# An attention and MLP-mixer kernel on Trainium2: other places in the queues for the loads and the last matmuls of one weight

## The chip, the core and the metric

The kernel runs on one core of a Trainium2 chip. A core has five engines that run side by side, each with its own queue of instructions that it takes in order: TensorE (PE, matrix products; its weight loads are shown as PEld), VectorE (DVE), ScalarE (ACT), GpSimd (POOL) and SyncE (SP), which here only issues transfers. Engines wait for each other through semaphores. An instruction at the head of a queue that still has to wait holds everything behind it. The metric is the time of one execution in microseconds (us).

## The reference

Three stages in a row, all in fp32, on batches of 2 and a sequence of 448:

```python
# 1. causal attention, 12 heads of 64
scores = where(mask, -1e9, q @ k.T / sqrt(64))
attn   = exp(scores - max(scores));  attn /= sum(attn) + 1e-9
x      = (attn @ v) laid out as [batch, 448, 768]
# 2. token and channel mixer
h  = relu(x.T @ w_tok1) @ w_tok2           # 448x256, 256x448, over tokens
u  = x + h.T
x  = u + relu(u @ w_ch1) @ w_ch2           # 768x1536, 1536x768, over channels
# 3. gated MLP
h  = gelu_tanh(x @ w_in);  a, g = halves of h        # 768x1024
gated = a * (w_sg @ layernorm(g) * g_ln + b_sg)      # over tokens, 448x448
out = x + gated @ w_out
```

The weights of stage 2 arrive as 64-bit floats.

## The kernel before

Precision is kept by splitting each fp32 operand into a high and a low part and taking three products, high x high, high x low and low x high (`mm3`, L184 to L188). A 64-bit weight slice is loaded as raw words by SP (`wraw`, L113) and decoded on the chip: ScalarE converts the upper words (L127), VectorE shifts and joins the lower ones (L130, L131), ScalarE makes the high part `whi` (L140) and GpSimd the low part `wlo` (L101). There are two buffers for raw slices, three for the joined `wm`, three for `whi` and `wlo`.

Attention goes over 24 heads, 12 of batch 0 and then 12 of batch 1, in pairs. A head is worked off in two halves. For a half, PE makes a tile of scores S (`s_ps`, L345), VectorE adds the mask and takes the maxima (L350), ScalarE makes the bias from the maxima (L357) and the exponentials (L359) and casts them to 16 bits (L371), GpSimd makes the low part (L372), and SP transposes both by a DMA (L373, `pT<-hl`). PE then multiplies the transposed tile `pT` with V (L396 to L398; `x_ps`, 15 matmuls for a half). The scores of the next halves are made ahead of these products, so that the chain from maximum to transpose has time. After the products of two heads VectorE divides by the sums (`rd`, `xf`, L424 to L426), and ScalarE and GpSimd split the result into `xh` and `xl` (L429, L101, L435).

After every fourth head `token_mix` runs the token mixer for those 256 channels: 22 matmuls with w_tok1 (`a_ps`, L443, L444 and mm3), a relu and split (`ah`, `al`, L448), 20 matmuls with w_tok2 and transposes of x (`u_ps`, L459), and a split of the sum into `u_hi`, `u_lo` (L470).

When batch 0 is through attention, its u is complete, and the first product of the channel mixer can start for batch 0 while batch 1 is still in attention. Its result has 12 tiles; the first eight of batch 0, m = 0 to 7, are made beside the heads of batch 1. One is called an R tile here: 18 matmuls on one decoded slice `w_ch1[m]` (`r_ps`). `up_third` (L493) makes tiles 0 to 3 in thirds of six matmuls between heads, `up` (L512) makes tiles 4 to 7 whole after the loop over heads. All of this is written in program order; a list scheduler that models time then places instructions on the queues, and three things steer it: `tc.high_priority` shifts an instruction's rank, the number of buffers sets the earliest place, and `tc.issue_after(x)` puts the instructions in its block behind x in the order of issue. The last is an order only, and acts on the queues of the engines that the block uses.

The loads of the eight slices are steered by such a block. `marks[n]` is the transpose (on SP) of head n's last half; the load of slice m stands behind `marks[H - 2 + m]`, which is head 10 + m. Without this the scheduler would place loads as early as their buffers allow.

From the R tiles on, batch 0 and 1 run the rest of the channel mixer and the gated MLP, with PE as the engine that everything waits for.

Of the kernel before, what the change touches and what calls it, by code (L numbers as in the profile page):

```python
# [28 lines left out]
def mixer_kernel(  # L29
# [20 lines left out]
    H, D = 2 * H2, D2 // 2  # L50
# [4 lines left out]
    NQ = 4  # L55
# [6 lines left out]
    AHEAD = 4  # L62
    VAHEAD = 2
    LATER = 1500

    def f32(ap):
        return ap.bitcast(F32)
# [75 lines left out]
    def load_w(src, pool=wpool, bufs=3):  # L143

        k = src.shape[1]
        hi = pool.tile([P, WC // P, P], F32R, tag="whi", name="whi", bufs=bufs)[:, :k, :]
        lo = pool.tile([P, WC // P, P], F32R, tag="wlo", name="wlo", bufs=bufs)[:, :k, :]
        load64(hi.rearrange("p a f -> p (a f)"), lo.rearrange("p a f -> p (a f)"), src.rearrange("p a f -> p (a f)"))
        return hi, lo
# [31 lines left out]
    def mm3(ps, pairs, begun=False, ended=True):  # L181

        n, done = len(pairs), []
        for i, ((lh, ll), (rh, rl)) in enumerate(pairs):  # L184
            nc.tensor.matmul(ps, lh, rh, start=i == 0 and not begun, stop=False)  # L185
            nc.tensor.matmul(ps, lh, rl, start=False, stop=False)  # L186
            done.append(nc.tensor.matmul(ps, ll, rh, start=False, stop=ended and i == n - 1).ins)  # L187
        return done  # L188
# [26 lines left out]
    def tok(i):  # L215
        return slice(KW[i] - rows(i), KW[i])
# [3 lines left out]
    def channel_up(m, batches, pool, psum):  # L220

        wh, wl = load_w(w_ch1[m])
        for b in batches:
            us = slice(b * S, (b + 1) * S)
            pr = psum.tile([P, 512], F32, tag="d", name="r_ps")
            mm3(pr[:, :S], [((wh[:, c, :], wl[:, c, :]), (u_hi[c][b], u_lo[c][b])) for c in range(NCC)])
            r_done(m, b, pr, pool)

    def r_done(m, b, pr, pool):

        r = pool.tile([P, S], F32, tag=f"r{m}_{b}", name="r")
        nc.scalar.activation(r, pr[:, :S], AF.Relu, accum_out=rsum[:, b, m:m + 1])
        r_of[m, b] = r
# [17 lines left out]
    with ExitStack() as at:  # L251
# [12 lines left out]
        w1h = tokw.tile([P, NQ, T], F32R, name="w1h")  # L264
        w1l = tokw.tile([P, NQ, T], F32R, name="w1l")
# [172 lines left out]
        def token_mix(b, g, xf, xh, xl):  # L438
            N = GH * D
            pa = ps_a.tile([P, NT, N], F32, tag="a", name="a_ps")  # L440
            for t in range(NT):
                ts = slice(t * P, (t + 1) * P)
                nc.tensor.matmul(pa[:, t, :], w1h[:, 0, ts], xh[:, 0, :], start=True, stop=False)  # L443
                nc.tensor.matmul(pa[:, t, :], w1l[:, 0, ts], xh[:, 0, :], start=False, stop=False)  # L444
                mm3(pa[:, t, :], [((w1h[:, c, ts], w1l[:, c, ts]), (xh[:, c, :], xl[:, c - 1, :])) for c in range(1, NQ)], True)
            ah = xp.tile([P, NT, N], F32R, tag="ah", name="ah")
            al = xp.tile([P, NT, N], F32R, tag="al", name="al")
            nc.scalar.activation(ah, pa, AF.Relu)  # L448
            nc.vector.scalar_tensor_tensor(al, pa, 0.0, f32(ah), ALU.max, ALU.subtract)

            ws = slice(64, 64 + S) if b == 0 else slice(0, S)
            for e in range(N // P):
                cc = g * (N // P) + e
                cs = slice(e * P, (e + 1) * P)
                pu = ps_u.tile([P, 512], F32, tag="u", name="u_ps")
                first = True
                for t in range(NT):
                    for l, r in ((ah, w2h), (ah, w2l), (al, w2h)):
                        nc.tensor.matmul(pu[:, :S], l[:, t, cs], r[:, t, ws], start=first, stop=False, skip_group_check=True)  # L459
                        first = False  # L460
                nc.tensor.matmul(pu[:, b * 64:b * 64 + 64], xh[:, 0, cs], ident2, start=False, stop=False, skip_group_check=True)
                for c in range(1, NQ):
                    xc = xf[:, e, 2 * c - 1:2 * c + 1].rearrange("p h d -> p (h d)")
                    if b == 1 and c == NQ - 1:
                        o, idn = pu[:, :S].rearrange("p (a t) -> p a t", t=64)[:, ::6], ident_s
                    else:
                        o, idn = pu[:, b * 64 + tok(c).start:b * 64 + tok(c).stop], ident
                    nc.tensor.matmul(o, xc, idn, is_transpose=True, start=False, stop=c == NQ - 1, skip_group_check=True)
                us = slice(b * S, (b + 1) * S)
                nc.scalar.copy(u_hi[cc][b], pu[:, :S])  # L470
                nc.vector.tensor_sub(u_lo[cc][b], pu[:, :S], f32(u_hi[cc][b]))


        last, last_x, marks = [None], [None], []
        order = [(b, h) for b in range(B) for h in range(H)]
        qks, vss = {}, {}

# [14 lines left out]
        dense = list(range(NF0))  # L492
        thirds = []  # L493

        def up_third():

            if not thirds:
                m = dense.pop(0)
                with tc.issue_after(marks[H - 2 + m]), tc.high_priority(offset=-LATER):
                    wh, wl = load_w(w_ch1[m])  # L500
                pr = ps_e.tile([P, 512], F32, tag="d", name="r_ps")
                thirds.extend((m, pr, wh, wl, c) for c in range(0, NCC, 2))
            m, pr, wh, wl, c0 = thirds.pop(0)
            mm3(
                pr[:, :S],
                [((wh[:, c, :], wl[:, c, :]), (u_hi[c][0], u_lo[c][0])) for c in (c0, c0 + 1)],
                c0 > 0, not thirds,
            )
            if not thirds:
                r_done(m, 0, pr, rpool)  # L510

        def up():  # L512

            m = dense.pop(0)
            with tc.issue_after(marks[H - 2 + m]):
                channel_up(m, [0], rpool, ps_e)

        def decode_tok(c):
# [12 lines left out]
        for n, (b, h) in enumerate(order):  # L531
            if n > 0:
                prepare(n + AHEAD)
                prepare_v(n + VAHEAD)
            if n == GH - 1:
                for c in range(2, NQ):
                    load_tok(c)
                for c in range(NT):
                    load_tok2(c)
            if h % GH == 0:  # L540
                x = (
                    xp.tile([P, GH // 2, 7, D], F32, tag="xf", name="xf", bufs=2),
                    xp.tile([P, NQ, GH * D], F32R, tag="xh", name="xh"),
                    xp.tile([P, NQ - 1, GH * D], F32R, tag="xl", name="xl"),
                )
            if h % 2 == 0:
                it = pair(b, h // 2, h % GH // 2, qks[b, h // 2], x, b == 0 and h > 0)
            next(it, None)
            marks.append(last[0])
            if h % GH == GH - 1:  # L550
                token_mix(b, h // GH, *x)

            if b == 1 and h >= 3:
                for _ in range(1 if h < H - 3 else 2):
                    up_third()

        while dense:
            up()


    NDC = 4
# [348 lines left out]
```

## Time and profile before

| | |
|---|---|
| median of 3 timed runs | 416.0 us (414.38 to 416.13) |
| the profiled execution | 416.44 us, span 414.7 us |
| mean granted clock of TensorE | 0.988 |
| PE busy | 391.3 us, 94% of the span |
| DVE, ACT, POOL busy | 282.4, 250.4 and 202.5 us (68, 60 and 49%) |

The span runs from the first to the last instruction in the trace; 1.7 us of the profiled execution lie around it. Busy times of PE are those of overlapping matmuls counted once. A share of 94% is a mean over stages: where PE is full, no other engine's work costs anything; where it has gaps, the wait that ends last there counts. The granted clock is the share of full speed that TensorE was given; 1.00 is 2.4 GHz, and a value between 0.5 and 1.00 for a stretch is a mean over time at 2.4 and at 1.2 GHz.

### The profile page before, as it was taken

To read this page: it belongs to the slowest core of one execution; us is meant where nothing else is said; L and a number is where in the kernel's file an instruction comes from. 1 tells how busy PE (TensorE), PEld (TensorE's weight loads), DVE (VectorE), ACT (ScalarE), POOL (GpSimd) and SP (SyncE) were. 2 spreads that over 40 slices of the span, in tenths; PEclk is the share of its full clock that TensorE was granted. 3 is DMA by queue.
4 is the path that set the end of the run, shared out by engine and by line. 5 is a ranking of instruction groups with operands and counts; after the bars stand their busy time and mean duration, and the time that the engine had idled before them with its cause. 6 is when DMAs were issued, how large, how long until landed. Compare 5 with 4: busy or idle time off the path is not lost.

```text
span 414.7 us, 7332 instructions
## 1 busy us (share of the span) xinstructions
PE 391.3 (94%) x2622; PEld 267.9 (65%) x2622; DVE 282.4 (68%) x696; ACT 250.4 (60%) x483; POOL 202.5 (49%) x208
## 2 busy tenths in 40 slices
PE   5879899799898998999999999999999999999996
PEld 3447778588787887999889555555544445554554
DVE  6887866887785426444446787557898996469742
ACT  3988767787876555565679886344256556553210
POOL 3759864997686466062261447145121348315300
PEclk9999999799999999999999999999999999999999
DMA  7999899979997544466643313534623131100122
GB/s 220 246 238 232 161 206 271 246 186 236 265 247 140 137 112 144 163 217 229 207 149 102 90 65 114 186 107 134 222 73 90 51 103 51 52 2 0 68 92 107
DMA packets 61747, 61.77 MB, mean 149 GB/s; under 512 B 47888, under 2 KB 53264, under 8 KB 61712
## 3 DMA queue, kind: packets, MB, share of 16 engines
q1 hardware_dynamic: 61712, 61.32, 55.6%
q8 instruction: 20, 0.33, 0.3%
q14 instruction: 15, 0.12, 0.1%
HBM read 47.29 MB, written 2.75 MB: 121 GB/s over the span
## 4 chain that ended last, share of the span: by engine, by line
PE 25%; DVE 18%; ACT 12%; POOL 10%; DMA 9%; issue 8%; SPq 0%; POOLq 0%; ACTq 0%
DMA wraw<-in 7%; PE r_ps L186 5%; PE r_ps L185 5%; PE r_ps L187 5%; ACT r L172 3%; POOL hl L372 3%; PE o_ps L187 2%; PE o_ps L185 2%; PE o_ps L186 2%; DVE y L173 2%; DVE wm L131 2%; DVE w2m L131 1%; ACT wm L127 1%; PE u_ps L459 1%; POOL w L179 1%
## 5 line engine op out<-in xcount | busy, mean ns | idle before, releaser
L345 PE MATMUL s_ps<-k,q 128*128 128x64 f32 (+3 forms) x216 | 57.2, 405 | 11.5 <-DVE mx L350 4.8
L372 POOL TENSOR_TENSOR hl<-pe,hl 128x512 f16<-128x512 f32 x43 | 52.3, 1223 | 25.6 <-ACT hl L371 24.5
L101 POOL TENSOR_TENSOR wlo<-wm,whi 128x768 fp32r<-128x768 f32 x20 | 39.9, 1994 | 40.4 <-ACT whi L140 40.2
L185 PE MATMUL r_ps<-uh,whi 128*128 128x448 f32 x144 | 55.1, 383 | 0.0
L130 DVE TENSOR_SCALAR wm<-wm 128x768 int32<-128x768 int32 (+2 forms) x35 | 22.9, 655 | 46.9 <-ACT wm L127 46.9
L186 PE MATMUL r_ps<-ul,whi 128*128 128x448 f32 x144 | 53.9, 374 | 0.0
L187 PE MATMUL r_ps<-uh,wlo 128*128 128x448 f32 x144 | 53.0, 368 | 0.0
L185 PE MATMUL y_ps<-r,w 128*128 128x448 f16 x144 | 50.8, 353 | 0.0
L127 ACT ACTIVATE wm<-wraw 128x768 f32<-128x768 f32 (+2 forms) x35 | 27.8, 798 | 38.0 <-DMA wraw<-in 24.1
L186 PE MATMUL y_ps<-r,w 128*128 128x448 f16 x144 | 50.7, 352 | 0.0
L187 PE MATMUL y_ps<-r,w 128*128 128x448 f16 x144 | 50.6, 352 | 0.0
L345 PEld LDWEIGHTS s_ps<-k,q 128*128 128x128 f32 x216 | 32.2, 207 | 22.5 <-DVE mx L350 6.7
L350 DVE CUSTOM_DVE_ANT_0 pe<-s_ps,mask 128x192 f32<-128x192 f32 (+3 forms) x84 | 34.6, 441 | 7.2 <-PE s_ps L345 6.4
L246 POOL TENSOR_TENSOR y<-yt,ul 128x448 f32<-128x448 f32 x12 | 15.8, 1319 | 46.4 <-DVE yt L244 46.4
L359 ACT ACTIVATE pe<-pe,bias 128x448 f32<-128x448 f32 (+3 forms) x74 | 35.6, 525 | 0.4
L131 DVE SCALAR_TENSOR_TENSOR wm<-wraw,wm 128x768 int32<-128x768 int32 (+2 forms) x35 | 32.8, 938 | 0.7
L396 PE MATMUL x_ps<-vh,pT 128*128 128x65 f16 (+1 forms) x240 | 26.9, 201 | 3.1 <-DMA pT<-hl 3.0
L371 ACT CAST hl<-pe 128x512 f16<-128x512 f32 x43 | 26.3, 611 | 5.9 <-DMA pT<-hl 4.7
L185 PEld LDWEIGHTS r_ps<-uh,whi 128*128 128x128 f32 x144 | 27.3, 190 | 3.0 <-issue 0.4
L186 PEld LDWEIGHTS r_ps<-ul,whi 128*128 128x128 f32 x144 | 27.2, 189 | 3.1 <-issue 0.6
L187 PEld LDWEIGHTS r_ps<-uh,wlo 128*128 128x128 f32 x144 | 27.2, 189 | 2.7 <-issue 0.2
L179 POOL TENSOR_TENSOR w<-w2m,w 128x768 f16<-128x768 f32 x12 | 21.2, 1787 | 15.8 <-ACT w L178 11.2
(212 smaller groups left out, 1016.0 us busy)
## 6 DMA issues: line engine op xcount, KB each, us to landing
wraw<-in SPq DMA_DIRECT2D x36, 768.0 KB, 4.5
wraw<-in SPq DMA_DIRECT2D x14, 512.0 KB, 3.8
vr<-in SPq DMA_DIRECT2D x12, 320.0 KB, 4.0
k<-in SPq DMA_DIRECT2D x12, 224.0 KB, 3.7
q<-in SPq DMA_DIRECT2D x24, 112.0 KB, 4.0
out<-ob SPq DMA_DIRECT2D x11, 224.0 KB, 1.9
wraw<-in SPq DMA_DIRECT2D x3, 256.0 KB, 4.6
pT<-hl SPq DMA_TRANSPOSE x43, 4.0
```

Source lines behind the costliest of these rows:

```text
L101: nc.gpsimd.tensor_sub(lo, src, f32(hi))
L127: nc.scalar.activation(m, words.bitcast(F32)[:, :, 1], AF.Prelu, scale=2.0 ** -112, alpha=-(2.0 ** 32))
L131: nc.vector.scalar_tensor_tensor(mi, words[:, :, 0], 29, mi, ALU.logical_shift_right, ALU.bitwise_or)
L185: nc.tensor.matmul(ps, lh, rh, start=i == 0 and not begun, stop=False)
L186: nc.tensor.matmul(ps, lh, rl, start=False, stop=False)
L187: done.append(nc.tensor.matmul(ps, ll, rh, start=False, stop=ended and i == n - 1).ins)
L345: last_s[0] = nc.tensor.matmul(ps[:, o:o + m], qp[:, q0:q0 + P], k2[:, ks], start=True, stop=True).ins
L350: last_mx[0] = nc.vector.tensor_tensor_reduce(out=pe[:, cs], in0=ps[:, cs], in1=mask0 if i == 0 else mask[:, MASKS[i]], scale=-1.0 / math. ...
L359: nc.scalar.activation(pe[:, cs], pe[:, cs], AF.Exp, bias=bias[:, j:j + 1], scale=-1.0)
L371: nc.scalar.copy(hl[:, 0], pe)
L372: nc.gpsimd.tensor_sub(hl[:, 1], pe, hl[:, 0])
L396: nc.tensor.matmul(o, ph, vh[:, c, h, :D + 1], start=j == 0, stop=False)
```

## The change

A table `BEHIND` gives the head behind whose last transpose each of the eight loads of w_ch1 for batch 0 is queued: 12, 15, 17, 18, 19, 20, 21, 22 in place of 10, 11, ..., 17. And the last two whole R tiles (m = 6 and 7) get a place on PE: the matmuls of m = 6 stand behind the last product with V (`last_x[0]`), those of m = 7 behind the last product with w_tok1 (`last_a[0]`, which is newly recorded). The computation is the same.

```diff
--- before.py
+++ after.py
@@ -62,6 +62,7 @@
     AHEAD = 4
     VAHEAD = 2
     LATER = 1500
+    BEHIND = [12, 15, 17, 18, 19, 20, 21, 22]
 
     def f32(ap):
         return ap.bitcast(F32)
@@ -442,7 +443,8 @@
                 ts = slice(t * P, (t + 1) * P)
                 nc.tensor.matmul(pa[:, t, :], w1h[:, 0, ts], xh[:, 0, :], start=True, stop=False)
                 nc.tensor.matmul(pa[:, t, :], w1l[:, 0, ts], xh[:, 0, :], start=False, stop=False)
-                mm3(pa[:, t, :], [((w1h[:, c, ts], w1l[:, c, ts]), (xh[:, c, :], xl[:, c - 1, :])) for c in range(1, NQ)], True)
+                amm = mm3(pa[:, t, :], [((w1h[:, c, ts], w1l[:, c, ts]), (xh[:, c, :], xl[:, c - 1, :])) for c in range(1, NQ)], True)
+            last_a[0] = amm[-1]
             ah = xp.tile([P, NT, N], F32R, tag="ah", name="ah")
             al = xp.tile([P, NT, N], F32R, tag="al", name="al")
             nc.scalar.activation(ah, pa, AF.Relu)
@@ -471,7 +473,7 @@
                 nc.vector.tensor_sub(u_lo[cc][b], pu[:, :S], f32(u_hi[cc][b]))
 
 
-        last, last_x, marks = [None], [None], []
+        last, last_x, last_a, marks = [None], [None], [None], []
         order = [(b, h) for b in range(B) for h in range(H)]
         qks, vss = {}, {}
 
@@ -496,7 +498,7 @@
 
             if not thirds:
                 m = dense.pop(0)
-                with tc.issue_after(marks[H - 2 + m]), tc.high_priority(offset=-LATER):
+                with tc.issue_after(marks[BEHIND[m]]), tc.high_priority(offset=-LATER):
                     wh, wl = load_w(w_ch1[m])
                 pr = ps_e.tile([P, 512], F32, tag="d", name="r_ps")
                 thirds.extend((m, pr, wh, wl, c) for c in range(0, NCC, 2))
@@ -509,10 +511,10 @@
             if not thirds:
                 r_done(m, 0, pr, rpool)
 
-        def up():
+        def up(behind=None):
 
             m = dense.pop(0)
-            with tc.issue_after(marks[H - 2 + m]):
+            with tc.issue_after(marks[BEHIND[m]]), tc.issue_after(behind) if behind else nullcontext():
                 channel_up(m, [0], rpool, ps_e)
 
         def decode_tok(c):
@@ -555,7 +557,7 @@
                     up_third()
 
         while dense:
-            up()
+            up({2: last_x[0], 1: last_a[0]}.get(len(dense)))
 
 
     NDC = 4
```

The queue of SP in the middle of attention, from the transposes of the first halves of a pair of heads on. `k2` and `q0` are loads for a later pair, `wraw` raw slices of w_ch1, `pT` transposes. Before:

```order
L113 DMA wraw_1667<-in_5 128x768
L113 DMA wraw_1932<-in_5 128x768
...
L298 DMA k2_1463<-in_1 128x448
L373 DMA_TRANSPOSE pT_1343<-hl_1344 128x8x128
L373 DMA_TRANSPOSE pT_1378<-hl_1379 128x8x128
L300 DMA q0_163<-in_0 64x448
L113 DMA wraw_2228<-in_5 128x768
L373 DMA_TRANSPOSE pT_1404<-hl_1405 128x8x128
L373 DMA_TRANSPOSE pT_1433<-hl_1434 128x8x128
```

After (its lines are numbered one or two higher):

```order
L299 DMA k2_1463<-in_1 128x448
L374 DMA_TRANSPOSE pT_1343<-hl_1344 128x8x128
L374 DMA_TRANSPOSE pT_1378<-hl_1379 128x8x128
L301 DMA q0_163<-in_0 64x448
L114 DMA wraw_1667<-in_5 128x768
L374 DMA_TRANSPOSE pT_1404<-hl_1405 128x8x128
L374 DMA_TRANSPOSE pT_1433<-hl_1434 128x8x128
```

The slices m = 0 (`wraw_1667`) and m = 1 (`wraw_1932`) stood ahead of four transposes more than now; m = 0 has the place of m = 2 (`wraw_2228`), and m = 1 and m = 2 come further down.

The queue of ScalarE in the same place: `wm` is the conversion of a slice, `bias`, `pe` and `hl` the steps of a half head, `uh` and `xh` splits of the token mixer, `vh` of V. Before:

```order
L371 CAST hl_1405<-pe0_155 128x512
L127 ACTIVATE wm_1666<-wraw_1667 128x768
L357 ACTIVATE bias_1429<-mx_1423 128x2
L359 ACTIVATE pe_1422<-pe_1422,bias_1429 128x192
L359 ACTIVATE pe_1422<-pe_1422,bias_1429 128x320
L371 CAST hl_1434<-pe_1422 128x512
L470 CAST uh2_0_98<-u_ps_932 128x448
L127 ACTIVATE wm_1931<-wraw_1932 128x768
```

After:

```order
L372 CAST hl_1405<-pe0_155 128x512
L358 ACTIVATE bias_1429<-mx_1423 128x2
L360 ACTIVATE pe_1422<-pe_1422,bias_1429 128x192
L360 ACTIVATE pe_1422<-pe_1422,bias_1429 128x320
L372 CAST hl_1434<-pe_1422 128x512
...
L322 ACTIVATE vh1_177<-vr_1316,sv_1322 128x10x64
L128 ACTIVATE wm_1666<-wraw_1667 128x768
L358 ACTIVATE bias_1487<-mx_1482 128x2
```

The conversion of slice 0 has moved from ahead of one half head's bias to ahead of the next one's (`bias_1487`), and that of slice 1 has left this place.

The end of attention on PE: `x_ps` are the last products with V, `r_ps_2544` and `r_ps_2575` the R tiles m = 6 and 7, `a_ps` the products with w_tok1, `u_ps` those with w_tok2. Before:

```order
L398 MATMUL x_ps_2248<-vh1_177,pT_2375 128x65
L186 MATMUL r_ps_2544<-ul4_0_114,whi_2534 128x448
L187 MATMUL r_ps_2544<-uh4_0_102,wlo_2535 128x448
...
L185 MATMUL r_ps_2575<-uh0_0_94,whi_2565 128x448
...
L187 MATMUL r_ps_2575<-uh5_0_104,wlo_2566 128x448
L443 MATMUL a_ps_2405<-xh_2083,w1h_151 128x256
...
L187 MATMUL a_ps_2405<-xh_2083,w1l_152 128x256
L459 MATMUL u_ps_2432<-w2h_153,ah_2428 128x448
```

After:

```order
L399 MATMUL x_ps_2248<-vh1_177,pT_2375 128x65
L186 MATMUL r_ps_2544<-uh0_0_94,whi_2534 128x448
...
L188 MATMUL r_ps_2544<-uh5_0_104,wlo_2535 128x448
L444 MATMUL a_ps_2405<-xh_2083,w1h_151 128x256
...
L188 MATMUL a_ps_2405<-xh_2083,w1l_152 128x256
L186 MATMUL r_ps_2575<-uh0_0_94,whi_2565 128x448
...
L188 MATMUL r_ps_2575<-uh5_0_104,wlo_2566 128x448
L461 MATMUL u_ps_2432<-w2h_153,ah_2428 128x448
```

Before, 13 matmuls of m = 6 stood ahead of the last products with V and five of m = 6 and 18 of m = 7 behind them; now 18 of m = 6 stand behind them, and the 18 of m = 7 between the products with w_tok1 and those with w_tok2.

## Rows read from the trace of the kernel before

**Rows 1.** The page's busy tenths in 40 slices of the span, PE.

```profile
PE   5879899799898998999999999999999999999996
```

**Rows 2.** Windows: us, busy us (x count) of PE PEld DVE ACT POOL, PEclk, DMA share, GB/s.

```profile
70.00:84.50 14.50, 12.15 (x119) 9.46 (x118) 12.13 (x36) 11.79 (x25) 12.16 (x14) 0.76 1.10 261
84.50:104.70 20.20, 20.20 (x202) 16.74 (x200) 15.23 (x41) 15.26 (x34) 16.79 (x21) 1.00 0.89 207
...
155.00:169.00 14.00, 12.17 (x83) 10.70 (x82) 7.15 (x9) 5.89 (x11) 7.57 (x8) 1.00 0.56 170
169.00:240.00 71.00, 71.00 (x356) 59.80 (x355) 39.40 (x76) 51.84 (x98) 26.78 (x14) 1.00 0.51 163
```

**Rows 3.** Timeline of PE: start, us, engine, line, out<-in [idle before <-releaser].

```profile
75.75 1.02 PE L345 MATMUL s_ps<-k,q 128*128 128x448 f32 x2 [2.00 <-DVE mx L350]
```

**Rows 4.** Timeline of SP's queue, 63 to 101 us.

```profile
63.77 1.05 SPq L113 DMA_DIRECT2D wraw<-in  x2
...
67.08 5.50 SPq L373 DMA_TRANSPOSE pT<-hl  x2
...
73.38 0.47 SPq L113 DMA_DIRECT2D wraw<-in  x1
73.94 4.76 SPq L373 DMA_TRANSPOSE pT<-hl  x2
...
87.63 4.97 SPq L373 DMA_TRANSPOSE pT<-hl  x3
...
99.22 1.06 SPq L113 DMA_DIRECT2D wraw<-in  x2
100.40 6.57 SPq L373 DMA_TRANSPOSE pT<-hl  x2
```

**Rows 5.** Timeline of ScalarE, 68 to 79 us.

```profile
68.93 0.91 ACT L127 ACTIVATE wm<-wraw 128x768 f32<-128x768 f32 x1 [1.69 <-DMA wraw<-in]
...
75.73 0.20 ACT L357 ACTIVATE bias<-mx 128x2 f32<-128x2 f32 x1
...
78.89 0.90 ACT L127 ACTIVATE wm<-wraw 128x768 f32<-128x768 f32 x1 [2.02 <-DMA wraw<-in]
```

**Rows 6.** Timeline of VectorE, near 70 us.

```profile
69.87 0.56 DVE L130 TENSOR_SCALAR wm<-wm 128x768 int32<-128x768 int32 x1 [2.48 <-ACT wm L127]
```

**Rows 7.** Tiles: pT whole, pT from 99 to 108 us, wraw whole.

```profile
L373 SPq DMA_TRANSPOSE pT<-hl x43: 1231/1247/4565, 11.2 to 148.5; - x43
...
DMA to landing us min/median/max: 3.0/4.0/9.1
...
DMA to landing us min/median/max: 8.1/8.6/9.1
...
DMA to landing us min/median/max: 3.1/4.3/7.1
```

**Rows 8.** Timeline of PE: four waits.

```profile
109.51 0.20 PE L396 MATMUL x_ps<-vh,pT 128*128 128x65 f16 x1 [1.69 <-DMA pT<-hl]
...
133.39 0.20 PE L396 MATMUL x_ps<-vh,pT 128*128 128x65 f16 x1 [1.31 <-DMA pT<-hl]
...
161.22 0.39 PE L443 MATMUL a_ps<-xh,w1h 128*128 128x256 f32 x1 [0.68 <-POOL xh L101]
...
165.54 0.48 PE L459 MATMUL u_ps<-w2h,ah 128*128 128x448 f32 x1 [0.69 <-ACT ah L448]
```

**Rows 9.** Lines, 60 to 170 us: xcount | busy, mean ns | idle before, releasers.

```profile
L101 POOL TENSOR_TENSOR wlo<-wm,whi 128x768 fp32r<-128x768 f32 x11 | 20.9, 1903 | 6.8 <-ACT whi L140 6.5
...
L131 DVE SCALAR_TENSOR_TENSOR wm<-wraw,wm 128x768 int32<-128x768 int32 x13 | 15.8, 1213 | 0.2
...
L127 ACT ACTIVATE wm<-wraw 128x768 f32<-128x768 f32 x13 | 11.8, 908 | 13.2 <-POOL wlo L101 6.8 <-DMA wraw<-in 6.2
...
L140 ACT CAST whi<-wm 128x768 fp32r<-128x768 f32 x11 | 9.1, 825 | 1.1 <-DVE wm L131 0.6 <-PE r_ps L186 0.5
```

**Rows 10.** Timeline of GpSimd, near 159 us.

```profile
158.93 1.84 POOL L101 TENSOR_TENSOR wlo<-wm,whi 128x768 fp32r<-128x768 f32 x1
```

## The prediction

> **What bounds the kernel now.** I read the page's slices first [rows 1]. TensorE (PE) is full in most; where it isn't is at the start, which this change doesn't touch, and in single slices between about 70 and 170 us. Next I read the busy times by stage [rows 2]. From 169 us on PE has no idle microsecond for 71 us at a clock of 1.00; 356 matmuls in 71.00 us are 0.20 us each. From there on the order of the program is the same in both kernels, so time can only be won or lost ahead of that point, in the second half of attention: 70 to 169 us. There PE loses time in four places, and the reader is to see a different cause in each.
>
> First, 70.0 to 84.5 us: 12.15 us busy of 14.50, so 2.35 idle, at a granted clock of 0.76 of the full one [rows 2]. That is a mixture of its two levels, 2.4 and 1.2 GHz; PE had waited 2.00 us for the maxima of score tiles (L350 on VectorE) [rows 3] before the slow time. 0.24 of 14.50 us are 3.5 us of full-speed work that wasn't done. The place costs 2.35 + 3.5 = 5.8 us. The reason stands on the other queues. SP issued two slices of w_ch1 at 63.77 [rows 4]; ScalarE's queue then stood 1.69 us at its conversion of the first one (L127) until that load landed, with a bias and exponentials of a running head queued behind it, and VectorE 2.48 us at the next step of the same slice (L130) [rows 5, 6]. A third slice, issued at 73.38, held ScalarE another 2.02 us at 78.89, in front of a head's cast (L371) [rows 4, 5]. The two transposes begun at 67.08 took SP 5.50 us, where the median transpose takes 1.25 [rows 4, 7].
>
> Second, near 107 us PE waited 1.69 us for a transposed tile pT [rows 8]. Two slices had gone out at 99.22, directly ahead of two transposes at 100.40 [rows 4]; those landed 8.1 and 9.1 us after their issue, the median being 4.0 [rows 7]. Third, near 133: 1.31 us, again for a pT [rows 8]. Fourth, 155 to 169: 14.00 - 12.17 = 1.83 us [rows 2], in waits after the last products with V: 0.68 for xh, 0.69 for ah [rows 8], and the rest, 0.46, for xl between them.
>
> **The change part by part.** No instruction is added or removed; eight loads, what decodes them, and two R tiles (18 matmuls each) move.
>
> *Loads behind later heads.* In the first place the two loads at 63.77 go, and the first slice is issued at the place of the third, between two pairs of transposes. What leaves this stretch is, twice over, one slice's decode: 0.91 (L127) and 0.83 (L140) on ScalarE, 0.56 (L130) and 1.21 (L131) on VectorE, 1.90 (L101) on GpSimd [rows 6, 9]; and the two waits of 1.69 and 2.48 us. But one wait stays, and I work it out. SP's transposes start at 67.08 as before; unheld they take 2 x 1.25, and the q load behind them 0.8 (67.08 + 5.50 to 73.38), so the first slice is issued at about 70.4 and lands, at the median of 4.3 [rows 7], near 74.7. L127 stands in ScalarE's queue ahead of the bias of the next head and ends near 75.6; that bias ran at 75.73 before [rows 5]. So the first half of this head gains nothing there. What gains is everything behind: the third slice's wait of 2.02 us in front of its cast goes, so the casts come 1.5 us sooner for the first half, and more for the second, whose cast stood behind a further L140. PE meanwhile has 60 matmuls with V and 22 with w_tok1 to do, for which it needn't wait for the new head. I take 3.5 of the 5.8 us. Its ends: 5.8, if the clock doesn't fall at all; and -2.0, if the slice lands later and ScalarE stands as long as at 78.89 while nothing covers it.
>
> In the second place the pair at 99.22 is gone: one transpose now stands ahead of the third slice, the next one behind a single slice. I take 1.2 of the 1.69 us; ends 0 (the transposes stay as late as now; with fewer loads in front they have no reason to be later) and 1.69.
>
> In the third place and up to 155 us the loads become denser, since the last five slices stand behind heads 18 to 22. Every load still has a transpose queued behind it on SP, and the last head's transpose now has two in front. I leave the wait of 1.31 us where it is.
>
> *The last two R tiles.* The seventh tile had 13 of its 18 matmuls ahead of the last products with V; now all 18 stand behind them. That takes 13 x 0.20 = 2.6 us of cover from the last transpose. In the kernel before nothing waited there. The last cast now has the eighth slice's L127 and the seventh's L140 just ahead of it, so the transpose will be later; I charge 1.0 us, with 0 and 2.6 as ends (the nearest row is the 1.31 us of the third place).
>
> The tail: before, 23 R matmuls (4.6 us) stood between the last V product and the products with w_tok1 (call them A); they covered all but 0.68 us of the chain rd, xf, xh, which so took 5.3. Now 18 stand there (3.6 us). The chain itself changes: a wlo of 1.84 us stood between the two halves of xh on GpSimd [rows 10]; now it stands ahead of all of them and can run while VectorE still makes xf. VectorE has one more L131 (1.21) in its way. So xh should be ready 5.3 - 1.84 = 3.5 to 4.7 us after the last V product, a wait of 0 to 1.1; with what is left of the 0.46 for xl I take 0.6 us in place of 1.15. The eighth tile now stands between A and the products with w_tok2 (U), 3.6 us over a wait of 0.69: that wait goes. 1.83 - 0.6 = 1.2 us gained; ends 0 and 1.8.
>
> **The sum.** -3.5 - 1.2 + 1.0 - 1.2 = -4.9 us. The profiled execution took 416.44 us (span 414.7), so 411.5 by that; from the median of the three timed runs, 416.0, it is 411.1. I take 411.3.
>
> By the Trainium skill (DMA: Bandwidth & Descriptors, section Queues, rings and completion order) each DMA engine takes the descriptors of a ring in the order in which they were put there. The 8.1 and 9.1 us of the second place agree with it. By that rule a transpose behind a slice pays for that slice wherever the slice stands, and since all eight still stand in front of transposes it speaks against this change; what it would give here is the second rival.
>
> **The rivals.** *All of it goes* (chance 0.15). If the clock stays at 1.00 through 70 to 85 us and the later loads collide with nothing, the four places give 5.8 + 1.69 + 1.31 + 1.83 = 10.6 us: 405.8. For it speaks that the other engines have slack: VectorE, ScalarE and GpSimd are busy 15 to 17 of 20.2 us in a stretch where PE is full [rows 2]. Against it: one slice still lands in the first stretch in front of a head.
>
> *Spread, not removed* (0.20). The heads of batch 1 stand behind the same eight decodes, in the same in-order queues, and each slice delays the next transposes. The first place then gives back later what it gains, since PE, once ahead, runs into pT tiles that come no sooner: three transposes in a row took SP 4.97 us at 87.63 with no slice near [rows 4], so attention's own pace is not far from PE's. Only the tail's 1.2 us stays, less the 1.0: 416 us. For it also: the single slice at 73.38 ahead of a pair of transposes went with 4.76 us on SP for the two [rows 4].
>
> *Late weights* (0.10), the case on the other side. From issue to wlo a slice needs 4.3 + 0.91 + 0.56 + 1.21 + 0.83 + 1.90 = 9.7 us [rows 6, 7, 9], and PE eats one R tile in 3.6. A tile whose slice is issued only two tiles' time ahead (7.2 us) waits 2.5 us. The last five loads stand behind five heads in a row, so the tiles of slices five to eight could each wait about 1.7: 6.8 us lost and 1.0 at the last transpose, against 3.5 + 1.2 won earlier and nothing left of the tail's gain: 3 us slower, 419. It decides if PE waits over 6 us in sum between the fourth tile and the first whole tile of batch 1. Against it: before, with loads far ahead, ScalarE waited 6.8 us in this stretch for GpSimd to free buffers [rows 9], so some of the lead was not used.
>
> **How the numbers follow.** Forecast 0.50, its own range 408.5 to 414; the three rivals 0.15, 0.20, 0.10; 0.05 lies between the first rival and the forecast. Half a per cent, about what a measurement of this kernel can tell from no change, is 2.1 us: faster is below 413.9, slower above 418.1. Faster: nearly all of the forecast, the first rival and the rest, 0.67. Same: the second rival and the forecast's upper end, 0.23. Slower: 0.10. The range for 8 in 10 reaches to the first two rivals: 406 to 416.3.
>
> **What would show it.** Right: no wait of ScalarE at L127 near 69 us; PE idle plus slow clock at 70 to 85 under 3 us; the wait for pT near 107 us shorter than 0.5; no wait for ah before the last U; PE full from about 164 us on, 5 us sooner than 169. Wrong: ScalarE standing at L127 for more than 3 us near 73 to 76 us, a second half-clock stretch between 75 and 100 us, or PE waiting for a wlo or for the last pT longer than 2.6 us. The forecast falls as a whole if the last U ends within 1 us of 169 us, or later.

## The result: slower, and the profile after

The changed kernel takes 419.6 us (median of 5 runs, 417.87 to 420.44) against 415.6 for the kernel before in the same comparison: ratio 1.0104, 95% interval 1.0082 to 1.0126. On another chip, in e9 below, it is 1.0118 (1.0063 to 1.0172). It is 1% slower where 1.1% faster was forecast. The profiled execution has a span of 417.6 us, 2.9 more than before. Medians and ratios here and below leave out the few executions that ran in a slower state (one each of e1, e6, e9 and e12, two of e8).

The page's slices of the kernel after, busy tenths of PE and the granted clock, to be read beside [rows 1]:

```profile
PE   5879889998988977999999999999999999999996
PEclk9989999999998996999999999999999999999999
```

The dip that stood in slice 8 has gone; a deeper one has come in slices 15 and 16. Busy times by stage of the kernel after (us, then busy us and count of PE, PEld, DVE, ACT, POOL, then PEclk, DMA share, GB/s):

```profile
70.00:84.50 14.50, 13.78 (x152) 11.47 (x151) 11.52 (x42) 11.02 (x26) 10.77 (x16) 1.00 0.97 200
84.50:104.70 20.20, 18.84 (x192) 15.33 (x191) 13.18 (x42) 15.12 (x38) 14.36 (x19) 1.00 0.90 181
104.70:130.00 25.30, 22.15 (x210) 19.04 (x210) 17.36 (x39) 19.64 (x41) 18.29 (x20) 0.96 0.87 196
130.00:150.50 20.50, 20.50 (x170) 17.85 (x169) 11.72 (x21) 11.73 (x22) 13.37 (x12) 0.97 0.91 237
150.50:171.50 21.00, 16.38 (x87) 14.84 (x82) 6.29 (x11) 8.24 (x15) 10.80 (x9) 0.84 0.50 168
171.50:242.50 71.00, 71.00 (x357) 59.90 (x356) 41.53 (x76) 51.53 (x98) 26.47 (x14) 1.00 0.49 162
```

and the stages of the kernel before that [rows 2] doesn't have:

```profile
104.70:130.00 25.30, 23.49 (x199) 20.09 (x198) 19.77 (x48) 19.59 (x45) 18.55 (x20) 1.00 1.05 235
130.00:155.50 25.50, 24.19 (x219) 21.42 (x218) 9.44 (x22) 14.81 (x31) 14.17 (x13) 1.00 0.58 119
155.50:168.80 13.30, 11.47 (x74) 10.11 (x70) 6.95 (x9) 5.89 (x11) 7.07 (x8) 1.00 0.51 169
```

The last products with V end at 150.5 us after and 155.5 before: 5.0 us sooner. 2.6 of these are the 13 R matmuls that now stand behind them (13 x 0.20), so by these two profiles attention itself won 2.4. From there to the first R tile of batch 1 it takes 21.0 us against 13.3. With 0.20 us for each of the 36 R matmuls in it (23 before), what isn't R takes 13.8 against 8.7: 5.1 lost. -2.4 + 5.1 = +2.7 of the 2.9 us. The 5.1 us repeat: e9, the same kernel in another execution, takes 21.1 us for that stretch. The 2.4 don't: seven kernels whose queues have the same order up to that point (the kernel after, e9, e1, e2, e3, e13 and e14 below) reached the last product with V between 148.8 and 154.5 us, so a gain of 2.4 from one profile isn't shown. What is clear of that spread is the loss at the end of attention.

PE's waits from 148 to 172 us in the kernel after (engine, line, waited for: us in total, times, longest), where the kernel before waited 0.68 for xh and 0.69 for ah [rows 8] and, as the last line here shows, 0.47 for xl:

```profile
PE a_ps L444 <- POOL xh L102: 3.7, 1, 3.7
PE a_ps L187 <- POOL xl L102: 0.9, 1, 0.9
```

```profile
162.31 0.39 PE L186 MATMUL a_ps<-xl,w1h 128*128 128x256 f32 x1 [0.47 <-POOL xl L101]
```

The chain behind the longer one stands on three queues. Timelines of the kernel after (start, us, engine, line, out<-in [idle before <-releaser]); VectorE:

```profile
153.23 0.56 DVE L131 TENSOR_SCALAR wm<-wm 128x768 int32<-128x768 int32 x1 [3.15 <-ACT wm L128]
153.71 0.22 DVE L425 TENSOR_SCALAR rd<-x_ps,sv 128x7 f32<-128x7 f32 x1
153.84 0.95 DVE L132 SCALAR_TENSOR_TENSOR wm<-wraw,wm 128x768 int32<-128x768 int32 x1
154.71 0.19 DVE L426 RECIPROCAL rd<-rd 128x7 f32<-128x7 f32 x1
154.94 0.62 DVE L427 TENSOR_TENSOR xf<-x_ps,rd 128x448 f32<-128x448 f32 x1
```

ScalarE:

```profile
152.29 0.91 ACT L128 ACTIVATE wm<-wraw 128x768 f32<-128x768 f32 x1 [2.71 <-DMA wraw<-in]
153.10 0.82 ACT L141 CAST whi<-wm 128x768 fp32r<-128x768 f32 x1
```

GpSimd:

```profile
154.00 2.45 POOL L102 TENSOR_TENSOR wlo<-wm,whi 128x768 fp32r<-128x768 f32 x1 [1.81 <-ACT whi L141]
156.42 0.56 POOL L436 TENSOR_SCALAR xh<-xf 64x64 fp32r<-64x64 f32 x2
157.06 1.08 POOL L102 TENSOR_TENSOR xh<-xf,xh 64x64 fp32r<-64x64 f32 x2
```

The conversion at 152.29 is that of the third slice loaded for batch 1; its R tile comes only at about 178.7 us (171.5 and two tiles of 3.6). Its raw words landed 2.71 us after ScalarE was ready for it. VectorE's next step of the same slice stands ahead of rd, so rd starts 3.2 us after the last product with V. Behind the conversion on ScalarE stands the whi of the first such slice, and GpSimd's wlo waits for that whi, ahead of xh's rows. In the kernel before rd started within 0.3 us of that product (155.55):

```profile
155.78 0.22 DVE L424 TENSOR_SCALAR rd<-x_ps,sv 128x7 f32<-128x7 f32 x1 [1.68 <-PE x_ps L398]
```

PE did R tile m = 6 in the meantime, then stood. Two stretches of the kernel after, and the first matmul of A and the first behind A, show the rest of the loss:

```profile
150.50:158.20 7.70, 3.99 (x27) 3.33 (x22) 3.06 (x7) 4.39 (x8) 5.59 (x6) 1.00 0.72 246
158.20:165.40 7.20, 6.28 (x26) 5.85 (x27) 1.77 (x3) 1.96 (x4) 3.36 (x2) 0.53 0.35 118
```

```profile
158.19 0.39 PE L444 MATMUL a_ps<-xh,w1h 128*128 128x256 f32 x1 [3.71 <-POOL xh L102]
164.09 0.57 PE L186 MATMUL r_ps<-uh,whi 128*128 128x448 f32 x1
```

After a stretch in which it was busy 3.99 of 7.70 us, TensorE ran at 0.53 of its full clock for 7.2 us. The waits are 4.63 us in place of 1.84, which is 2.8 more. The 22 matmuls of A took 5.0 us without their wait for xl (158.19 to 164.09, less 0.92); in the kernel before they took 3.2 at a clock of 1.00 (161.22 to 164.85, less 0.47). The first three R matmuls behind A took 0.37 us each in place of 0.20. That is 1.8 + 0.5 = 2.3 us for the slow clock, and 2.8 + 2.3 = 5.1, what was lost.

What ScalarE's conversions waited for tells why the slices are late. Its group in the kernel after, 60 to 172 us (count | busy, mean ns | idle before and releasers):

```profile
L128 ACT ACTIVATE wm<-wraw 128x768 f32<-128x768 f32 x13 | 11.7, 902 | 17.8 <-DMA wraw<-in 14.4 <-POOL wlo L102 3.4
```

In [rows 9] the same group waited 6.8 us for GpSimd (a buffer) and 6.2 for loads. Now it waits 14.4 for loads: the lead of the loads was used up.

### The profile page after: what moved, and what is told of

Read it like the earlier page. It is cut to its first block, busy times and chain, and to the rows that moved or that the text cites. A ratio compares the mean times of both kernels' runs of the same rounds, so it can differ in the third digit from the quotient of the medians.

```text
span 417.6 us, 7332 instructions
## 1 busy us (share of the span) xinstructions
PE 391.7 (94%) x2622; PEld 268.9 (64%) x2622; DVE 281.8 (67%) x696; ACT 250.3 (60%) x483; POOL 202.3 (48%) x208
## 4 chain that ended last, share of the span: by engine, by line
PE 29%; DVE 19%; DMA 16%; POOL 13%; ACT 12%; issue 10%; SPq 0%; POOLq 0%; ACTq 0%; DVEq 0%
DMA wraw<-in 10%; DMA pT<-hl 4%; PE r_ps L188 4%; PE r_ps L186 4%; PE r_ps L187 4%; ACT r L173 3%; PE s_ps L346 3%; POOL hl L373 3%; PE o_ps L188 2%; PE o_ps L187 2%; PE o_ps L186 2%; DVE pe L351 2%; DVE y L174 2%; DVE wm L132 2%; DVE w2m L132 1%
## 5 line engine op out<-in xcount | busy, mean ns | idle before, releaser
L131 DVE TENSOR_SCALAR wm<-wm 128x768 int32<-128x768 int32 (+2 forms) x35 | 23.2, 664 | 41.8 <-ACT wm L128 41.8
```

## The experiments

Three theories: A, the loss is made at the end of attention, where decodes of slices that land late stand ahead of rd and xh; B, it is the cover that the two R tiles took away; C, it is made earlier, by the first loads, in new waits between 75 and 130 us. Each ratio is to the kernel before on the same chip, with its 95% interval.

| run | loads behind heads | tiles placed | time, us | ratio |
|---|---|---|---|---|
| e9, the kernel after | 12, 15, 17, 18, 19 to 22 | yes | 420.0 | 1.0118 (1.0063 to 1.0172) |
| e3 | the same | no | 419.3 | 1.0097 (1.0062 to 1.0133) |
| e10 | the same, the eighth behind 21 | yes | 419.9 | 1.0108 (1.0055 to 1.0161) |
| e4 | 10 to 17, as before | yes | 416.0 | 1.0005 (0.9974 to 1.0037) |
| e5 | 10 to 13, 19 to 22 | yes | 416.1 | 1.0009 (0.9988 to 1.0031) |
| e6 | 12, 15, 17, five times 18 | yes | 414.4 | 0.9959 (0.9929 to 0.9988) |
| e11 | as e6 | no | 415.5 | 0.9995 (0.9962 to 1.0028) |
| e2 | as after, rd ahead on VectorE | yes | 422.3 | 1.0148 (1.0107 to 1.0189) |
| e13 | as after, xh ahead on GpSimd | yes | 420.4 | 1.0083 (1.0050 to 1.0116) |
| e14 | as after, both | yes | 417.6 | 1.0040 (1.0006 to 1.0074) |
| e1 | as after, both and ScalarE | yes | 416.8 | 1.0022 (0.9990 to 1.0053) |
| e7 | as before, all three | yes | 415.5 | 0.9993 (0.9964 to 1.0021) |
| e8 | as e6, all three | yes | 415.3 | 0.9990 (0.9956 to 1.0023) |
| e12 | as e6, the fifth slice's decode later | yes | 420.1 | 1.0105 (1.0050 to 1.0161) |

**The two halves of the change.** e3 leaves out the places of the tiles, e4 leaves out the later loads:

```diff
# e3, from the kernel after
-            up({2: last_x[0], 1: last_a[0]}.get(len(dense)))
+            up()
# e4, from the kernel after
-    BEHIND = [12, 15, 17, 18, 19, 20, 21, 22]
+    BEHIND = [10, 11, 12, 13, 14, 15, 16, 17]
```

> The kernel after with the loads behind later heads, and no place given to the last two R tiles: on PE the 18 matmuls of m = 7 stand between the last products with V and A, m = 6 stays where it is. Theory A: the late chain is the same (xh ready 7.6 us after the last product with V), but 3.6 us more of R cover it; PE waits under 1 us for xh, about 1 us for xl and 0.7 for ah, and TensorE isn't slowed: 413 to 415. Theory B: the loads by themselves gain what was forecast for them, 411 to 412.

> The kernel before with the places of the two last R tiles alone; the loads stand behind heads 10 to 17. Theory A: the slices have landed long before, so rd isn't held, xh comes 4 to 5.5 us after the last product with V; PE waits up to 1.9 us for it in place of 0.68 and not for ah: 415 to 417, the same as before. Theory B: the cover of 3.6 us is gone and with it 3 us: 418 to 420.

The loads alone make the whole loss, the tiles alone none that the interval shows. e4 came out as theory A had it; PE's waits there, 148 to 172 us:

```profile
PE a_ps L187 <- POOL xl L102: 1.0, 1, 1.0
PE a_ps L444 <- POOL xh L102: 0.8, 1, 0.8
```

e3 missed both theories' numbers. The second tile does cover xh there, and TensorE isn't slowed, but the late chain shows behind it:

```profile
PE u_ps L461 <- ACT ah L450: 2.0, 1, 2.0
PE a_ps L187 <- POOL xl L102: 1.1, 1, 1.1
PE r_ps L186 <- ACT r L233: 0.9, 1, 0.9
```

4.0 us where I had said 2.7 at most. The rest of the miss (419.3 for 415) lies ahead of the last product with V, which came at 153.2 us there and at 150.5 in the kernel after with the same order ahead of it; it isn't explained by this.

**Which of the late loads.** e5, e6, e10, and e9, the kernel after once more:

```diff
# e5
+    BEHIND = [10, 11, 12, 13, 19, 20, 21, 22]
# e6
+    BEHIND = [12, 15, 17, 18, 18, 18, 18, 18]
# e10
+    BEHIND = [12, 15, 17, 18, 19, 20, 21, 21]
```

> The kernel after with the first four loads where the kernel before has them (behind heads 10 to 13) and the last four where the kernel after has them (19 to 22). Theory A (the loss is made at the end of attention: with the last loads late, rd on VectorE and xh's rows on GpSimd stand behind decodes of slices that land after the last product with V): rd starts 2 us or more after that product, PE waits over 2.5 us for xh, and the time is 418 to 421, as in the kernel after. Theory C (the loss is made by the first loads, in new waits for pT and xh between 75 and 130 us): 415 to 417.

> The kernel after with its first four loads behind heads 12, 15, 17, 18, and the last four behind 18 too, so that they go out as soon as buffers allow (the load of the third slice of batch 1 stands ahead of the last transpose in place of behind it). Theory A: rd is held under 1 us, PE waits under 1.5 us for xh, the time is 415 to 417. Theory C: the loss stays, 418 to 420.

> The kernel after once more, on one chip with the three that follow. Theory A says 418.5 to 420.5 for it.

> The kernel after with the eighth load alone one head earlier (behind 21 in place of 22); the third slice of batch 1 is still loaded behind the last transpose. Theory A (that slice's decode holds rd and the wlo ahead of xh's rows, whatever the eighth load does): rd still starts over 2 us after the last product with V, 418 to 420. If the eighth load's own place is what costs: 415 to 417.

e6 differs from the kernel after in four numbers, and it takes away the loss: its interval against before lies wholly below that of the kernel after. The third slice for batch 1 is now loaded ahead of the last transpose (issued at 144.0 and 144.4 us; in the kernel after 1.3 us behind it, at 147.7 and 146.4). In e6 ScalarE's conversion of it waits for a buffer and no longer for the load, and GpSimd's wlo starts 0.9 us after the last product with V (151.1) in place of 3.5. ScalarE, GpSimd and PE of e6:

```profile
149.96 0.90 ACT L128 ACTIVATE wm<-wraw 128x768 f32<-128x768 f32 x1 [1.43 <-POOL wlo L102]
```

```profile
152.04 2.11 POOL L102 TENSOR_TENSOR wlo<-wm,whi 128x768 fp32r<-128x768 f32 x1 [2.11 <-ACT whi L141]
```

```profile
155.91 0.39 PE L444 MATMUL a_ps<-xh,w1h 128*128 128x256 f32 x1 [0.63 <-POOL xh L102]
```

e10, in which that load still follows the last transpose, loses as the kernel after does. ScalarE and PE of e10:

```profile
153.41 0.91 ACT L128 ACTIVATE wm<-wraw 128x768 f32<-128x768 f32 x1 [2.20 <-DMA wraw<-in]
```

```profile
159.31 0.58 PE L444 MATMUL a_ps<-xh,w1h 128*128 128x256 f32 x1 [4.08 <-POOL xh L102]
```

e5 is a miss for theory A: the last four loads as late as in the kernel after, and no loss. Two things differ there. The scheduler put the decode whose load was late behind rd and xf on VectorE, so rd came 0.2 us after the last product with V (149.85), and GpSimd was done with xh's rows at 155.3, 5.5 us after it in place of 7.6. VectorE of e5:

```profile
150.08 0.22 DVE L425 TENSOR_SCALAR rd<-x_ps,sv 128x7 f32<-128x7 f32 x1
152.12 0.56 DVE L131 TENSOR_SCALAR wm<-wm 128x768 int32<-128x768 int32 x1 [0.93 <-ACT wm L128]
```

And it put one more R tile behind the last product with V (54 R matmuls to the first tile of batch 1, in place of 36); PE waited for nothing from 148 to 172 us. So late loads alone don't decide; it takes that their decode stands ahead of x's last steps. How much of it the longer cover did, e5 doesn't show.

**Which queue holds xh.** Four kernels are the kernel after with the decodes of batch 1's slices moved behind the last steps of x, by engine (the edit is one line in the kernel, broken here):

```diff
# e1: all three; e2: the first alone; e13: the third alone; e14: the first and the third
-            channel_up(m, [1] if m < NF0 else [0, 1], r1pool, ps_d)
+            with tc.issue_after(xf_of[0]) if m in (2, 3) else nullcontext(), \
+                    tc.issue_after(xh_of[0]) if m in (2, 3) else nullcontext(), \
+                    tc.issue_after(xl_of[0]) if m < 4 else nullcontext():
+                channel_up(m, [1] if m < NF0 else [0, 1], r1pool, ps_d)
```

(`xf_of`, `xh_of`, `xl_of` hold the last xf on VectorE, the last cast of xh on ScalarE, the last xl on GpSimd.)

> The kernel after with one edit: the decodes of the slices that follow in batch 1 stand behind the last xf (VectorE), the last cast of xh (ScalarE) and the last xl (GpSimd). Theory A (at the end of attention rd and xh stand in their queues behind decodes of later slices whose raw words haven't landed): the last products with V end at about the same 150.5 us as in the kernel after, rd starts within 0.5 us of that in place of 3.2 later, PE's wait for xh falls from 3.7 to under 0.7 us, TensorE isn't slowed in 158 to 165, and the time falls from 419.6 to 411 to 414. Theory B (the loss is the cover that the two moved R tiles took away, the chain rd, xf, xh is as long as it is): the wait for xh stays above 2.5 us, and the time at 418 to 420.

> The kernel after with VectorE's part of the edit alone: the decodes of the third and fourth following slice stand behind the last xf on VectorE; ScalarE and the order of wlo on GpSimd stay. Theory A: rd starts about 3 us sooner, but the wlo of the first following slice on GpSimd still stands ahead of xh's rows and waits for ScalarE's whi, which stands behind the late slice's conversion; so xh comes less than 1 us sooner and the time is 418.5 to 419.6. If rd alone held the tail, the time would fall to 412 to 414. Theory B: no change, 419 to 420, with rd sooner and nothing gained.

> The kernel after with GpSimd's part alone: the low parts (wlo) of batch 1's first slices stand behind the last xl; VectorE keeps the third slice's decode ahead of rd, ScalarE its conversion ahead of the last cast of xh. Theory A with two holds in parallel (rd behind the late decode on VectorE, xh's rows behind the late wlo on GpSimd): rd still starts about 3.2 us after the last product with V, xf ends 5.0 after it, xh is ready 6.7 after it in place of 7.6, PE still waits 2.5 to 3 us for it: 418 to 419.5. If GpSimd's hold is the only one that counts, the wait falls under 1 us: 415 to 417.

> The kernel after with VectorE's and GpSimd's part together, ScalarE's order kept ahead of the cast. Theory A: rd starts within 0.5 us of the last product with V and xh's rows aren't held; the cast on ScalarE still stands behind the third slice's conversion, so A starts 4 to 5 us after the last product with V in place of 7.7; PE waits under 1.2 us in all, TensorE isn't slowed there, and the time is 415 to 417.5, like that with all three parts (416.8). If ScalarE's hold counts as much as the others: 418 or more.

In e2 rd starts 0.7 us after the last product with V (149.3), and nothing is gained by it, which is what theory A expected, though the time is worse than it said: the wlo still stands ahead of xh's rows, and xl, which the scheduler now puts between them, makes it worse. The profile is of e2's fastest execution (417.8, median 422.3). VectorE, GpSimd and PE of e2:

```profile
150.02 0.21 DVE L425 TENSOR_SCALAR rd<-x_ps,sv 128x7 f32<-128x7 f32 x1
```

```profile
153.57 2.44 POOL L102 TENSOR_TENSOR wlo<-wm,whi 128x768 fp32r<-128x768 f32 x1 [1.75 <-ACT whi L141]
155.98 0.56 POOL L436 TENSOR_SCALAR xh<-xf 64x64 fp32r<-64x64 f32 x2
156.62 1.00 POOL L102 TENSOR_TENSOR xl<-xf,xh 128x384 fp32r<-128x384 f32 x1
```

```profile
159.26 0.58 PE L444 MATMUL a_ps<-xh,w1h 128*128 128x256 f32 x1 [5.50 <-POOL xh L102]
```

In e13 GpSimd is free and VectorE holds; rd comes 4.0 us after its product (152.7), and PE waits 3.3 us:

```profile
156.69 0.22 DVE L425 TENSOR_SCALAR rd<-x_ps,sv 128x7 f32<-128x7 f32 x1
```

```profile
160.03 0.58 PE L444 MATMUL a_ps<-xh,w1h 128*128 128x256 f32 x1 [3.27 <-POOL xh L102]
```

With both away (e14) what is left is ScalarE's part, the cast of xh behind the late conversion, and 0.8 for xl; 1.7 us in all where under 1.2 was expected, and TensorE was slowed there after all (0.51 from 158.6 to 162.0 us):

```profile
PE a_ps L186 <- ACT xh L430: 0.9, 1, 0.9
PE a_ps L187 <- POOL xl L431: 0.8, 1, 0.8
```

With all three away (e1) PE has no idle time from the last product with V to the first tile of batch 1:

```profile
154.50:167.90 13.40, 13.40 (x85) 12.48 (x81) 7.89 (x11) 7.66 (x15) 9.63 (x9) 1.00 0.50 161
```

So two holds lie side by side; with one away the other still makes PE wait 5.5 us (e2) and 3.3 (e13), and neither alone gives a gain clear of noise. The times follow: 422.3, 420.4, 417.6, 416.8, and the ratios, each to the kernel before on its own chip, in the same order. For e13 and e14 that is what theory A expected, within 1 us; for e2 it is worse; e1 misses its 411 to 414. Its end of attention is 7.6 us shorter than that of the kernel after (13.4 for 21.0), its time only 2.8 lower (3.4 by the ratios). From the first tile of batch 1 to the end it took 248.5 us in place of 246.1, which is 2.4 given back; the rest isn't settled, and in its profile the last product with V came only at 154.5.

Over all runs one sign goes with the loss. Where rd came 3.2 to 4.4 us after the last product with V (the kernel after, e9, e3, e10, e13), the time is 0.8 to 1.2% above that of the kernel before. Where it came within 0.3 us (e1, e4, e5, e6, e7, e8, e11, e14), it is at most 0.4% away from it, above or below. The exceptions are e2, where GpSimd holds xh alone, and e12.

**Whether attention gains.** e7 is e4 and e8 is e6, each with the edit of e1; e11 is e6 with that of e3; e12 is e6 with the decode of the fifth slice behind xf and xl of heads 4 to 7 of batch 1 (`up` makes that tile):

```diff
# e7, from e1
-    BEHIND = [12, 15, 17, 18, 19, 20, 21, 22]
+    BEHIND = [10, 11, 12, 13, 14, 15, 16, 17]
# e8, from e1
+    BEHIND = [12, 15, 17, 18, 18, 18, 18, 18]
# e11, from e6
-            up({2: last_x[0], 1: last_a[0]}.get(len(dense)))
+            up()
# e12, from e6: added to the with of up()
+            with tc.issue_after(xf_of[1, 3]) if m == 4 else nullcontext(), \
+                    tc.issue_after(xl_of[1, 3]) if m == 4 else nullcontext():
                 channel_up(m, [0], rpool, ps_e)
```

> The loads as before (behind heads 10 to 17), the two R tiles as after, and the decodes of batch 1's slices behind the last xf, xh and xl. Theory A: PE doesn't wait for xh, xl or ah at the end of attention; from the last product with V to the first R tile of batch 1 it takes 13.4 us in place of 17.1 in the run with the tiles alone, and the time falls by 2 to 3.5 us against that: 412.5 to 414. Theory C says nothing of it; if PE gives the gain back later it is 415 to 416.

> The same order of decodes with the loads behind heads 12, 15, 17 and five times 18. If the late first loads gain in attention what was forecast for them (4.7 us), and the end of attention has no wait, the time is 409 to 411. If they gain nothing there, because their waits come back as waits for pT at 75 us and for xh near 125 us, it is 413 to 416, no better than the same order of decodes with the loads as before.

> Loads behind heads 12, 15, 17 and five times 18, and no place given to the last two R tiles; on PE both stand between the last products with V and A. Theory A: R tiles of 7.2 us cover xh and xl, PE waits for ah 0.7 us: 413.5 to 415.5, the same as with the tiles placed. If placing the last tile between A and U gives the 0.7 us that was forecast: 0.5 to 1 us slower than with the tiles placed, 415 to 416.

> Loads behind heads 12, 15, 17 and five times 18, the two tiles placed, and the decode of the fifth slice behind the last xf (VectorE) and xl (GpSimd) of heads 4 to 7 of batch 1. PE waited 2.2 to 3.2 us for xh near 125 us in all runs with the first four loads late; there a step of that decode stood between rd and xf, and its wlo between the rows of xh. Theory A (a decode ahead of xf and xh holds PE in both places): that wait falls under 1 us, and the time by 1.5 to 3 us against 414.6: 411.5 to 413. If the wait comes back as one for pT: 414 to 415.

e7 and e8 repair the end of attention like e1 (about 13.4 us each) and end where the kernel before does; both times lie in the ranges that were written down for a gain given back, or none. Part of it is given back later: from the first tile of batch 1 to the end e7 took 249.7 us and e8 247.7, the kernel before 245.9. The stage behind, full in the kernel before, waits in both for a part of w_ch2 that GpSimd splits (1.4 and 1.3 us). e7, PE's waits from 165 us on:

```profile
PE y_ps L188 <- POOL w L180: 1.4, 1, 1.4
```

e11, 415.5, fits both its expectations, since it is about 1 us above e6; its wait for ah is 0.7 us, as said. e12 missed. VectorE is free there, but a wlo still stands ahead of xh's rows on GpSimd, as in e2, and the wait near 125 us stays. GpSimd and PE of e12:

```profile
118.73 2.17 POOL L102 TENSOR_TENSOR wlo<-wm,whi 128x768 fp32r<-128x768 f32 x1
120.87 1.27 POOL L436 TENSOR_SCALAR xh<-xf 64x64 fp32r<-64x64 f32 x2
```

```profile
124.52 0.58 PE L444 MATMUL a_ps<-xh,w1h 128*128 128x256 f32 x1 [2.65 <-POOL xh L102]
```

Why it is almost 6 us slower than e6 on top of that isn't settled; its profile is of its fastest execution, 416.6 us, and doesn't show it.

## Why the prediction was wrong

*The tail: this step failed.* The prediction gave it -1.2 us; it cost 5.1. It said of the wlo that now "it stands ahead of all of them and can run while VectorE still makes xf", and that xh would be ready 3.5 to 4.7 us after the last product with V. It took 7.7. I had priced the wlo and the extra L131 by their durations (1.84 and 1.21), as work that is ready to run. In the kernel before they were ready. In the kernel after the decode step on VectorE waits for a slice that is still on its way, and the wlo for a whi that stands behind that slice's conversion on ScalarE (2.71 us of waiting for the load); what waits at the head of a queue costs its wait. e2, e13, e14 and e1 show the two holds, e6 and e10 that the late load makes them. The last U ended at 171.5 us, by which the forecast falls as it had said itself. The 1.0 us charged for the last transpose didn't come: PE was busy for all of 130 to 150.5 us.

*U waits no more for ah: right.* The wait of 0.69 is gone in the kernel after. The tile between A and U is worth about that much or nothing: e11 and e6 differ by about 1 us, within their intervals.

*The rival that came true* is late weights, at 0.10 and 419 us. Its time was right by luck and its place wrong: I looked for PE waiting at a wlo of an R tile. PE never did; the slices hold xh, because their decodes share three queues with it. The argument against it, that ScalarE had waited for GpSimd's buffers and so some of the lead was unused, was weak: 6.2 us of waits for loads stood in the same row.

*The first place* came out as forecast in the profile of the kernel after: at 70 to 84.5 us 0.72 us idle at a clock of 1.00, so 5.1 of the 5.8 us. The wait at L127 near 69 us is gone and there is one of 1.07 us at 75.32, where 74.7 was worked out for the landing. But it was given back: 1.36 us idle at 84.5 to 104.7 (none before), 3.15 idle and a clock of 0.96 at 104.7 to 130 (1.81 idle before), 2.4 in all of the forecast 3.7 left by the last product with V. The largest new wait, 2.2 us for xh at 127 us, is the same pattern as in the tail, with the fifth slice, whose wlo (124.58, 1.81 us) stands between xh's rows. This is the rival of spread, not removed, in part.

The first place doesn't come out so in every execution. In the twelve kernels with the first four loads late the queues have the same order up to 85 us. In eight of them the first slice landed 4.9 to 5.4 us after its issue, and the clock stayed at 1.00 there. In e1, e3, e13 and e14 it took 6.6 to 7.4 us, ScalarE stood 3.1 to 3.6 us at its conversion, PE waited 2.8 to 3.2 us for pT, and the clock fell to half for 3.4 us. A slice that lands later was the condition that the forecast had named for its bad end; it had put the landing at the median, 4.3 us. PE of e1:

```profile
78.01 0.20 PE L397 MATMUL x_ps<-vh,pT 128*128 128x65 f16 x1 [2.84 <-DMA pT<-hl]
```

*The second place.* The wait of 1.69 us at 107 us is gone, as forecast. But four waits for pT with 2.6 us in all stand between 62 and 148 us, where before there were two with 3.0; with the same order, e9 has 2.0 and e3 4.8. The Trainium skill (DMA: Bandwidth & Descriptors, section Queues, rings and completion order) says that an engine takes a ring's descriptors in their order; by that rule the waits move with the slices and don't go, and the trace agrees in the main: between 60 and 150 us of the kernel after, the transposes issued while a slice was still on its way landed 3.1 to 7.1 us after their issue, 4.6 in the middle, and the others 3.1 to 4.5, 3.4 in the middle.

*The size of the first term* was read from one execution. Beside e1 to e4 the kernel before ran 23 times. In eight of these runs the mean granted clock was 0.999 or 1.000, so there was no slow stretch to speak of; they took 414.2 to 415.9 us, 414.8 in the middle, where the median of all was 415.4. So on the median most of the 3.5 us wasn't there to be won. e6, whose tail is as good as the kernel before's, puts what the later first loads are worth at 0.4%, 1.7 us, with an interval from 0.5 to 3.0; e8 and e11, with the same loads, show no gain clear of noise, so a gain of the first loads isn't settled. Nor do the profiles show one: e4 and e7, with the loads as before and 36 R matmuls behind it too, reached the last product with V at 151.3 and 154.0 us, the seven kernels named above at 148.8 to 154.5. That nothing changes behind 169 us held for this change (245.9 us before and 246.1 after from the first tile of batch 1 to the end), but not for e1, e7 and e8.

## What to carry over

Before a load is moved later, list what stands behind each step of its decode on every queue: a step whose data are late holds everything queued behind it, and the price is the wait, not the step's duration. When two queues hold the same result, taking one hold away can show nothing, so test them together as well as singly. A stage read from one profile needs a second execution before its term is carried. A lead that looks unused at the first consumer may be what keeps a later, unrelated chain free.

## What was not expected of the hardware

In the profiles of the kernel after, e9, e2 and e10, PE waited 3.7 to 5.5 us for xh at the end of attention, and TensorE's granted clock fell to about half for some 7 us (0.53 over 7.2 us in the kernel after; 0.51 from 156.2 to 163.0 in e9). In e13, with a wait of 3.3 us, it was 0.51 from 160.0 to 163.4. 0.5 of full speed is the lower of the two levels, 1.2 GHz. In e1, with no wait there, it stayed at 1.00. The length of the waits alone doesn't settle it: in e4 and e14, with two waits of 1.9 and 1.7 us in all, the clock was 0.51 for 3.4 us (from 158.2 and 158.6), in e6 and e12, with 1.7 and 1.9 us, it stayed at 1.00. By the sum above the slow stretch of the kernel after added 2.3 us to its waits of 4.63.
